# Mixed full and windowed attention on one core: transfer lists charged with measured issue times, lists of B's values queued only on a short SyncE backlog, and a new table of planner settings

## The chip, the cores and the metric

The kernel runs on one core of a Trainium2 chip. The metric is the device time of one execution in microseconds, lower is better. A core has a matrix engine (TensorE, PE in the profile), a vector engine (VectorE, DVE), an activation engine (ScalarE, ACT), GpSimd (POOL) and SyncE (SP), which here only issues DMA transfers. The engines run their own instruction lists and meet through semaphores.

## The reference

Two attentions over the same input x (2048 tokens, 640 features, bfloat16, 32 heads of 20 features) are mixed by a gate that is computed for each token. Attention A is full, without a mask; attention B lets every token see itself and seven earlier ones at distances 2, 4, ... 14.

```python
g = sigmoid((x * gate_w).sum(-1, keepdims=True))
# A: qkv = x @ A_wqkv;  p = softmax(q k^T * 20**-0.5);  a = (p v) @ A_wo
# B: qkv = x @ B_wqkv;  k, v gathered at pos - 2*w, w = 0..7 (masked below 0)
#    attn = softmax(q . k_w * 20**-0.5);  b = (sum_w attn_w v_w) @ B_wo
return g * a + (1 - g) * b
```

## The kernel before

**A planner writes the order.** The Python program that builds the kernel is a list scheduler. `_Sched.task` (called `T`) appends one instruction, or one list of DMA issues, to an engine's list and moves that engine's clock forward by a charged duration. For a DMA list it is given two charges: `dur`, after which the list's data are taken to be there, and `iss`, the time that SyncE is held by each of its `nd` issues (0.75 us where nothing is said). These charges never run on the chip. They only decide which instruction the planner puts next on which engine. On the chip each engine works through its list in that order and waits on semaphores where data are late.

**Attention A.** The work is 32 groups: 8 sets of four heads (q = 0 to 7) by 4 chunks of 512 queries. A group has 64 units, one for each of 16 blocks of 128 keys and each of the four heads. A unit is a score matmul (L1672), an exponential, and a matmul with V into `obank` (L1742). Units are put into tiles of two or three (`next_tile`, L1620), two tile buffers `score` taking turns. ScalarE computes the exponentials of a whole tile (`ebuf`, L1697). A tile of two can carry one more unit as a "ride": VectorE computes that exponential with integer arithmetic, first `uD` (L1687), and then, for four such units together, three shifted copies `eD` (L899). Both ways end in matmuls into `obank`. At the end of a group `gen_norm` transposes `obank` (L845), divides, and stores the result with a list of transfers `oTd<-oN` (L864).

**Side work.** Everything else is written as Python generators, which ask for a resource (`yield ("pe", ...)`, `("dve", ...)`, `("bank", ...)`) and are advanced by `step` (L1280) between two tiles, in `spend` (L1773), as far as the planner's clocks allow. `run_until` forces one of them forward where a tile needs its result. The generators that matter here:

- `gen_v` projects A's values, the first half of the heads in the order VORD, then the second half.
- `gen_q1` (L772) projects the queries of the first four heads for the query chunks 1 to 3. It writes |q| into `stg` (L783) as an input for a bound on the scores.
- `gen_kq` (L679) projects K and then Q for the other 28 heads in five shards f (six heads each, four in the last). For each shard: four K projections copied into `stg` (L698), a list of transfers into `kT` (L703), the largest |k| on VectorE (L707 to L718), four Q projections (L728), a list into `qT` (L733), and the bound from |q| and the largest |k| through `qbnd` into `qT` (L756). The weights of the next step are loaded into `WqP` by `w_load` (L674).
- `gen_bproj(u)` (L919) projects B's q, k and v for a unit u of 256 tokens (copies L945) and queues four lists of four transfers that spread v to the layout `vR` (L953).
- `gen_b(u)` (L958) multiplies q by k shifted (L971), sums, takes the softmax, sends the factors `rB` by transfers (L1054, L1056), multiplies the weights by `vR` (L1068), and sums into `oB`.
- `gen_wo` loads B's output weights (L604); `gen_fold` multiplies by the output weights and stores the result (L1259).

All these transfer lists go through SyncE's one queue, in the order in which the planner queued them. A list that waits for its data holds those behind it.

**The table.** `PLAN` holds a row of 18 settings for many tile numbers s (multiples of 5); from tile s on they hold until the next row. They are margins and priorities: how far a side matmul may run past a tile's limit (SLACK), when a third bank may be given to a tile (XTOL, XPRIO, XLATE), when VectorE may take a ride (DWAIT, DIDLE, DIDLE2, DTIME), the priorities of the shifted copies, how far VectorE may be booked ahead, when a filler matmul is put in (FILL), and how much earlier B's work is taken (BOFF). With other settings the order of the whole program is another.

Of the kernel before, what the change touches and what calls it, by code (L numbers as in the profile page):

```python
# [404 lines left out]
def _build(ctx, nc, A_x, A_wqkv, A_wo, B_wqkv, B_wo, gate_w, out):  # L405
# [266 lines left out]
    def w_load(part, f):  # L672
        d0, m = DH * heads[f][0], DH * len(heads[f])
        T("sp", 3.0, lambda e: e.dma_start(WqP[:, :, 0:m], wA_v[:, :, part * D + d0:part * D + d0 + m]), writes=WQ, dma=True)  # L674

    due = [99]
    kqn = [0]

    def gen_kq():  # L679
# [1255 lines left out]
```

## Time and profile before

| | before |
|---|---|
| median of 3 runs (lowest to highest) | 808.96 us (808.18 to 810.17) |
| profiled execution: time, span | 807.94 us, 806.1 us |
| granted TensorE clock, mean | 0.999 |
| TensorE busy | 746.2 us (93%) |
| VectorE busy | 741.8 us (92%) |
| ScalarE busy | 769.8 us (95%) |
| GpSimd busy | 92.5 us (11%) |
| exponentials on ScalarE, on VectorE | 1640 units in 725 tiles, 408 units |
| DMA | 32.6 MB, mean 40 GB/s |

The span runs from the first to the last instruction of the profiled execution; that execution's time is 1.84 us longer. An engine's idle time is the span less its busy time. Durations of instructions that follow one another on an engine overlap a little in the profile, so that the distance between starts can be shorter than the duration. A DMA list is seen on SP as so many issues; when it has landed is seen from the engine that waited for it.

### The profile page before, as it was taken

The numbers are of one execution on the slowest core, as the hardware profiler recorded it, in microseconds if no ns is written. First come the engines' busy times: TensorE is split into PE (matmuls) and PEld (weight loads), VectorE is DVE, ScalarE is ACT, GpSimd is POOL, SyncE is SP. The second block draws the span as 40 slices with busy tenths as digits, with TensorE's granted clock in tenths as the row PEclk, the third lists the DMA queues.
The fourth block names the chain that finished last, engine by engine and source line by source line (L and its number), as shares of the span: only waits on it lengthen the run. The fifth ranks groups of instructions, "written<-read, shape, count | busy, mean of one in ns | idle before, by whom it ended". The sixth has DMA issues, their size and how long they took to land.

```text
span 806.1 us, 27829 instructions
## 1 busy us (share of the span) xinstructions
PE 746.2 (93%) x11855; PEld 280.5 (35%) x11857; DVE 741.8 (92%) x1266; ACT 769.8 (95%) x757; POOL 92.5 (11%) x148
## 2 busy tenths in 40 slices
PE   8999998989999898989999998989899999999997
PEld 4323342334334233323343342333234333333322
DVE  7878998989999999999999999999999899999896
ACT  4999999989999999999999999999999999999996
POOL 3010001110020010101110100100021010111110
PEclk9999999999999999999999999999999999999999
DMA  8001110141030021101301320310212003000001
GB/s 261 26 24 31 26 33 6 38 85 29 6 76 11 5 44 38 22 22 40 76 13 38 78 54 22 74 27 6 64 28 65 5 17 81 22 23 23 23 21 35
DMA packets 47535, 32.61 MB, mean 40 GB/s; under 512 B 15029, under 2 KB 45653, under 8 KB 47413
## 3 DMA queue, kind: packets, MB, share of 16 engines
q1 hardware_dynamic: 47124, 30.51, 15.6%
q8 instruction: 94, 1.54, 0.8%
q10 hardware_dynamic: 288, 0.33, 0.1%
q14 instruction: 29, 0.23, 0.1%
HBM read 9.34 MB, written 2.62 MB: 15 GB/s over the span
## 4 chain that ended last, share of the span: by engine, by line
DVE 35%; PE 29%; ACT 15%; issue 10%; SPq 7%; DMA 3%; POOL 0%; POOLq 0%; DVEq 0%; ACTq 0%
ACT ebuf L1697 15%; DVE uD L1687 12%; PE score L1672 8%; PE obank L1742 8%; DVE eD L899 8%; PE side L651 7%; SPq L953 6%; DVE stage L971 3%; PE score L651 3%; DVE qkvB L945 2%; DVE stage L1068 2%; DMA stage<-qkvB 2%; DVE oTt L845 1%; DVE vA L814 1%; DMA qT<-stg 1%
## 5 line engine op out<-in xcount | busy, mean ns | idle before, releaser
L1697 ACT ACTIVATE ebuf<-score 128x1024 bf16<-128x1024 f32 (+1 forms) x725 | 758.1, 1184 | 19.6 <-PE score L1672 17.8
L1672 PE MATMUL score<-qT,kT 32*128 32x512 bf16 x2048 | 285.7, 384 | 31.5 <-ACT ebuf L1697 20.7
L1687 DVE TENSOR_SCALAR uD<-score 128x512 int16<-128x512 f32 x408 | 269.9, 682 | 17.1 <-PE score L1672 16.0
L899 DVE TENSOR_SCALAR eD<-uD 128x2048 int16<-128x2048 int16 x306 | 209.6, 706 | 3.8 <-PE obank L1742 3.0
L1742 PE MATMUL obank<-ebuf,vA 128*21 128x512 bf16 x1640 | 153.2, 385 | 9.5 <-DVE oTt L845 3.4
L1672 PEld LDWEIGHTS score<-qT,kT 32*128 32x128 bf16 x2048 | 70.7, 91 | 262.2 <-ACT ebuf L1697 172.0
L1742 PE MATMUL obank<-eD,vS 128*21 128x512 bf16 x1224 | 107.7, 380 | 1.2 <-DVE eD L899 1.2
L651 PE MATMUL side<-xT,wBs 128*32 128x256 bf16 x2400 | 96.2, 281 | 1.7 <-DVE qkvB L945 1.2
L851 POOL TENSOR_TENSOR rcp<-rcp,gA 128x16 f32<-128x16 f32 x31 | 7.5, 243 | 659.6 <-DVE rcp L849 659.6
L651 PEld LDWEIGHTS side<-xT,wBs 128*32 128x32 bf16 x2400 | 68.4, 142 | 29.7 <-issue 14.5
L1742 PEld LDWEIGHTS obank<-ebuf,vA 128*21 128x21 bf16 x1640 | 36.7, 89 | 92.6 <-issue 57.5
L1068 DVE TENSOR_TENSOR stage<-stage,eB 128x2048 bf16<-128x2048 bf16 x40 | 48.0, 1224 | 6.2 <-DMA stage<-qkvB 6.2
L651 PE MATMUL side<-xT,WqP 128*32 128x512 bf16 (+2 forms) x605 | 48.5, 382 | 2.0 <-DVE qkvB L945 0.9
L971 DVE TENSOR_TENSOR stage<-qkvB 128x2048 bf16<-128x2048 bf16 x40 | 47.8, 1230 | 0.1
L945 DVE CAST qkvB<-side 128x512 bf16<-128x512 f32 (+1 forms) x72 | 42.1, 594 | 3.0 <-PE side L651 2.8
L1742 PE MATMUL obank<-uD,vA 128*21 128x512 bf16 x408 | 39.6, 379 | 0.0
L890 POOL TENSOR_TENSOR vS<-vA,vw 128x252 bf16<-128x252 bf16 x55 | 37.0, 693 | 19.1 <-DVE maskB L594 13.2
L1742 PEld LDWEIGHTS obank<-eD,vS 128*21 128x21 bf16 x1224 | 29.9, 91 | 21.2 <-DVE eD L899 4.0
L858 POOL TENSOR_TENSOR oN<-oTt,rcp 128x512 bf16<-128x512 f32 x31 | 32.7, 1054 | 2.4
L845 DVE STREAM_TRANSPOSE oTt<-obank 128x512 f32<-128x512 f32 x32 | 22.8, 712 | 4.8 <-PE obank L1742 4.6
L651 PE MATMUL side<-xT,oTd 128*32 128x512 bf16 (+1 forms) x500 | 26.1, 304 | 0.0
L651 PEld LDWEIGHTS side<-xT,WqP 128*32 128x32 bf16 (+2 forms) x605 | 13.1, 94 | 19.8 <-issue 7.9
(200 smaller groups left out, 477.0 us busy)
## 6 DMA issues: line engine op xcount, KB each, us to landing
stage<-qkvB SPq DMA_DIRECT2D x128, 80.6 KB, 2.1
wBs<-in_B_wqkv_dram SPq DMA_DIRECT2D x1, 2400.0 KB
kT<-stg SPq DMA_DIRECT2D x28, 80.0 KB
qT<-stg SPq DMA_DIRECT2D x28, 80.0 KB
oTd<-oN SPq DMA_DIRECT2D x108, 20.0 KB
out_dram<-outsb SPq DMA_DIRECT2D x12, 160.0 KB
oTd<-in_A_x_dram SPq DMA_DIRECT2D x2, 640.0 KB
WqP<-in_A_wqkv_dram SPq DMA_DIRECT2D x8, 150.0 KB, 2.5
```

Source lines behind the costliest of these rows:

```text
L651: ins = e.matmul(o[j:k, :], l(j) if callable(l) else l[:, j:k], r, start=(first and i == 0), stop=(last and i == n - 1), skip_group_check= ...
L858: T(en, c2, lambda e: e.tensor_tensor(oo, ii, ib, ALU.mult), reads=["rcp", "oTt"], writes=["oN0"])
L890: T("pool", 0.607, lambda e: e.tensor_tensor(vS[:, i, :, :], _ap(vA[q // 4], (kb * 4 + q % 4) * 4 * DV, [[0, K - 1], [1, 4 * DV]]), _ap(vw ...
L899: T("dve", 0.065 + 0.1334 * n, lambda e, k=k, sl=sl: e.tensor_scalar(eD[:, sl % NS, 0:512 * n].bitcast(I16), uD[d % NU][:, 0:512 * n].bitc ...
L945: t = TB(dvc(n * TOK), lambda e, o=o, i=i: e.tensor_copy(o, i), reads=[("side", b)], writes=[key])
L953: T("sp", 2.0 + 0.65 * 4, lambda e, w4=w4, lo=lo: [e.dma_start(vR[32 * w4:32 * w4 + 32, a * CN:(a + 1) * CN, :], vB[32 * a:32 * a + 32, :, ...
L971: TB(dvc(CH, 2), lambda e: e.tensor_tensor(o, i0, i1, ALU.mult), reads=["qB", "kB"], writes=[("prod", i)] + ([("WkP", 0)] if u == 0 else [ ...
L1068: TB(dvc(CH, 2), lambda e: e.tensor_tensor(o, i0, i1, ALU.mult), reads=["eB"] + [("vR", w4) for w4 in range(4)], writes=[("prod", i)], por ...
L1672: ins = e.matmul(o, kT[32 * j:32 * j + 32, q % NQS, kb * P:(kb + 1) * P], qT[32 * j:32 * j + 32, q % NQS, GROUPS[g][0] * 512:(GROUPS[g][0] ...
L1687: t = T("dve", 0.598, lambda e: e.tensor_scalar(uD[d % NU][:, 512 * i:512 * (i + 1)].bitcast(I16), side[x], UOFF, 0.0, op0=ALU.add, op1=AL ...
L1697: exps[s] = T("act", actc(512 * n), lambda e: e.activation(ebuf[s % NE][:, 0:512 * n], score[s % 2][:, 0:512 * n], ACTF.Exp, scale=LN2 / S ...
L1742: ins = e.matmul(obank[32 * j:32 * j + DV, :], v, src, start=(kb == 0), stop=(last and k >= len(lst) - 4), skip_group_check=True)
```

## The change

It has five parts.

1. **Charges.** `dur` and `iss` of the transfer lists of `gen_kq`, of `vR`, of `rB` and of B's output weights get other numbers.
2. **WkQ.** K's weights of shard 0 are loaded at the start into a free part of `stage`. `gen_kq` begins when the first half of V and the query chunk 1 are projected (before: when all query chunks of `gen_q1` are). After the K half of shard 0 it waits for `gen_q1` to end, and goes on with Q, whose weights `gen_q1` loads last in place of K's. `gen_q1` uses `qbnd` for |q|, as `stg` is in use by then. `gen_b` waits for shard 0's K half, since its first product overwrites `WkQ`.
3. **The gate on vR lists.** Before each of the four lists `gen_bproj` asks for SyncE: the list is queued only when SyncE's planned backlog is at most 0.4 us.
4. **Order of B's projections.** The projection of v for unit u waits until the vR lists of unit u - 1 are queued.
5. **The table.** All rows of `PLAN` are replaced (its last row is at tile 725; before, at 720).

```diff
 PLAN = {
-    0: ((0.31, 0.76), 0.01, 1.0, 5.5, 0.94, -1.37, -0.5, 9.99, 7.0, 5.87, 0.67, 0.62, 5.69, 4.3, 0.0, 0.63, 2, -3),
...
-    720: ((0.34, 0.86), 0.16, 1.0, 5.5, 0.94, -1.14, -0.97, 9.86, 7.0, 8.62, 0.59, 0.62, 5.69, 5.04, 0.0, 0.54, 2, -3),
+    0: ((0.32, 0.64), 0.16, 2.5, 2.5, 0.94, -1.41, -0.97, 11.8, 7.0, 8.62, 0.67, 0.96, 4.4, 4.3, 0.0, 0.75, 2, -3),
...
+    725: ((0.48, 0.45), 0.25, 2.5, 5.5, 0.83, -2.18, -0.5, 5.48, 2.0, 6.06, 0.52, 0.47, 4.61, 3.44, 0.2, 0.52, 2, 0),
 }
...
# gen_wo
-              writes=[("woBp", f)] + (...), dma=True, iss=3.7)
+              writes=[("woBp", f)] + (...), dma=True)
...
+    WkQ = _ap(stage, 1024, [[DH * len(heads[0]), CN], [1, DH * len(heads[0])]])
+    T("sp", 3.0, lambda e: e.dma_start(WkQ, wA_v[:, :, D + DH * heads[0][0]:D + DH * heads[0][0] + DH * len(heads[0])]),
+      writes=["WkQ"], dma=True)
...
# gen_kq
-        while not done.get(("q", POS[QCN - 1, 0])):
+        while not (done.get(("v", VORD[-1], 0)) and done.get(("q", POS[1, 0]))):
             yield ("cond",)
         for f in range(CN):
+            Wk, wk = (WkQ, ["WkQ"]) if f == 0 else (WqP, WQ)
...
-                mms = [(side[b][0:m, :], WqP[:, c, 0:m], xT[:, c, cols]) for c in range(CN)]
-                yield from mm_group(b, mms, WQ + XT(tcc), mmc(512))
-                if tcc == 3:
+                mms = [(side[b][0:m, :], Wk[:, c, 0:m], xT[:, c, cols]) for c in range(CN)]
+                yield from mm_group(b, mms, wk + XT(tcc), mmc(512))
+                if tcc == 3 and f:
                     w_load(0, f)
...
# lists kT<-stg and qT<-stg
-            T("sp", 2.2 + 0.65 * len(hs), ... iss=0.65)
+            T("sp", 2.7 + 0.765 * len(hs), ... iss=0.765)
...
# after the K half of a shard
+            done[("k", f)] = True
+            while not done.get(("q", POS[QCN - 1, 0])):
+                yield ("cond",)
...
# list qT<-qbnd
-            T("sp", 2.2 + 0.65 * 4 * len(runs), ... iss=0.65)
+            T("sp", 2.4 + 0.55 * 4 * len(runs), ... iss=0.55)
...
# gen_q1
-                w_load(1, 0)
+                w_load(0, 0)
...
-                stg[:, cols].bitcast(U16), side[b][:, :].bitcast(U16)[:, 1:1024:2], 0x7FFF, None, op0=ALU.bitwise_and),
-              reads=[("side", b)], writes=[("stg", qc)])
-            yield from mm_group(b, [(side[b][:, :], KM[0], stg[:, cols])], [("KM", 0), ("stg", qc)], mmc(512), first=False)
+                qbnd[:, :].bitcast(U16), side[b][:, :].bitcast(U16)[:, 1:1024:2], 0x7FFF, None, op0=ALU.bitwise_and),
+              reads=[("side", b)], writes=["qbnd"])
+            yield from mm_group(b, [(side[b][:, :], KM[0], qbnd[:, :])], [("KM", 0), "qbnd"], mmc(512), first=False)
...
# gen_bproj
+            while u and m == 2 and f0 == 0 and not done.get(("bproj", u - 1)):
+                yield ("cond",)
...
         for w4 in range(4):
+            yield ("sp", 0.4)
             lo = PADB - DIL - 2 * DIL * w4
-            T("sp", 2.0 + 0.65 * 4, lambda e, w4=w4, lo=lo: [e.dma_start(
+            T("sp", 3.2 + 0.65 * 4, lambda e, w4=w4, lo=lo: [e.dma_start(
...
# gen_b
-        while not (done.get(("bqk", u)) and (u == 0 or done.get(("bs", u - 1)))):
+        while not (done.get(("k", 0)) and done.get(("bqk", u)) and (u == 0 or done.get(("bs", u - 1)))):
             yield ("cond",)
...
# lists of rB
-        T("sp", 2.0 + 0.5 * 4, ...
+        T("sp", 2.4 + 0.65 * 4, ...
-        spread = lambda: T("sp", 2.0 + 0.5 * 3, ...
+        spread = lambda: T("sp", 2.4 + 0.65 * 3, ...
...
# step
+        elif req[0] == "sp":
+            if not force and sch.avail["sp"] > now + req[1]:
+                return False
```

More of the change, by code (lines that the diff above doesn't have):

```diff
@@ L604, in gen_wo @@
             T("sp", 6.0, lambda e, f=f, src=src: e.dma_start(woBp[f], src) if f < CN - 1 else e.dma_start(woBp[f][:, :], src),
-              writes=[("woBp", f)] + ([("vA", kb, 0) for kb in range(KBN)] + [("vAones", 0)] if f == 0 else []), dma=True, iss=3.7)
+              writes=[("woBp", f)] + ([("vA", kb, 0) for kb in range(KBN)] + [("vAones", 0)] if f == 0 else []), dma=True)
             n = nchunk[0]
@@ L702, in gen_kq @@
             old = [k_ for q in qs if q >= NQS for tcc in range(4) for k_ in kT_keys(q - NQS, tcc)]
-            T("sp", 2.2 + 0.65 * len(hs), lambda e, hs=hs: [e.dma_start(
+            T("sp", 2.7 + 0.765 * len(hs), lambda e, hs=hs: [e.dma_start(
                 kT[32 * (h % 4) + 1:32 * (h % 4) + 1 + DH, h // 4 % NQS, :], stg[DH * i:DH * i + DH, :]) for i, h in enumerate(hs)],
-              reads=SG + [("kTz", q) for q in qs if q < NQS], writes=[("kTd", q, f) for q in qs] + old, dma=True, nd=len(hs), iss=0.65)
+              reads=SG + [("kTz", q) for q in qs if q < NQS], writes=[("kTd", q, f) for q in qs] + old, dma=True, nd=len(hs), iss=0.765)
             yield ("dve", DVE_AHEAD, sch.free(*SG))
@@ L732, in gen_kq @@
             old = [k_ for q in qs if q >= NQS for qc in range(QCN) for k_ in qkeys[POS[qc, q - NQS]]]
-            T("sp", 2.2 + 0.65 * len(hs), lambda e, hs=hs: [e.dma_start(
+            T("sp", 2.7 + 0.765 * len(hs), lambda e, hs=hs: [e.dma_start(
                 qT[32 * (h % 4) + 1:32 * (h % 4) + 1 + DH, h // 4 % NQS, :], stg[DH * i:DH * i + DH, :]) for i, h in enumerate(hs)],
-              reads=SG + [("qTz", q) for q in qs if q < NQS], writes=[("qTd", q, f) for q in qs] + old, dma=True, nd=len(hs), iss=0.65)
+              reads=SG + [("qTz", q) for q in qs if q < NQS], writes=[("qTd", q, f) for q in qs] + old, dma=True, nd=len(hs), iss=0.765)
             yield ("dve", DVE_AHEAD, sch.free(*SG))
@@ L755, in gen_kq @@
             runs = [(q, [i for i, h in enumerate(hs) if h // 4 == q]) for q in qs]
-            T("sp", 2.2 + 0.65 * 4 * len(runs), lambda e, runs=runs, hs=hs: [e.dma_start(
+            T("sp", 2.4 + 0.55 * 4 * len(runs), lambda e, runs=runs, hs=hs: [e.dma_start(
                 qT[32 * (hs[il[0]] % 4):32 * (hs[il[-1]] % 4) + 1:32, q % NQS, qc * 512:(qc + 1) * 512],
@@ L759, in gen_kq @@
               reads=["qbnd"] + [("qTz", q) for q in qs if q < NQS], writes=[("qTb", q, f) for q in qs] + old, dma=True,
-              nd=4 * len(runs), iss=0.65)
+              nd=4 * len(runs), iss=0.55)
             for q in qs:
@@ L951, in gen_bproj @@
         for w4 in range(4):
+            yield ("sp", 0.4)
             lo = PADB - DIL - 2 * DIL * w4
-            T("sp", 2.0 + 0.65 * 4, lambda e, w4=w4, lo=lo: [e.dma_start(
+            T("sp", 3.2 + 0.65 * 4, lambda e, w4=w4, lo=lo: [e.dma_start(
                 vR[32 * w4:32 * w4 + 32, a * CN:(a + 1) * CN, :], vB[32 * a:32 * a + 32, :, lo:lo + VW]) for a in range(4)],
-              reads=["vB"], writes=[("vR", w4)] + ([("WkP", 0)] if u == 0 and w4 == 0 else []), dma=True, nd=4, iss=0.65)
+              reads=["vB"], writes=[("vR", w4)], dma=True, nd=4, iss=0.65)
         done[("bproj", u)] = True
@@ L971, in q_chunk @@
             TB(dvc(CH, 2), lambda e: e.tensor_tensor(o, i0, i1, ALU.mult),
-               reads=["qB", "kB"], writes=[("prod", i)] + ([("WkP", 0)] if u == 0 else []), port=True)
+               reads=["qB", "kB"], writes=[("prod", i)] + ([("WkP", 0), "WkQ"] if u == 0 else []), port=True)
         def q_sum(f, b):
@@ L1052, in gen_b @@
            reads=["rQ", "tB"], writes=["rQ"])
-        T("sp", 2.0 + 0.5 * 4, lambda e: [e.dma_start(rB[0:32, j * TQ:(j + 1) * TQ], rQ[32 * j:32 * j + 32, :]) for j in range(4)],
+        T("sp", 2.4 + 0.65 * 4, lambda e: [e.dma_start(rB[0:32, j * TQ:(j + 1) * TQ], rQ[32 * j:32 * j + 32, :]) for j in range(4)],
           reads=["rQ"], writes=["rB"], dma=True, nd=4)
-        spread = lambda: T("sp", 2.0 + 0.5 * 3, lambda e: [e.dma_start(rB[32 * i:32 * i + 32, :], rB[0:32, :]) for i in range(1, 4)],
+        spread = lambda: T("sp", 2.4 + 0.65 * 3, lambda e: [e.dma_start(rB[32 * i:32 * i + 32, :], rB[0:32, :]) for i in range(1, 4)],
                            reads=["rB"], writes=["rB"], dma=True, nd=3)
```

262 rows, old and new, of the table PLAN are left out of this document.

## The prediction

> **What bounds the kernel now.** I read part 1 of the page first, then the groups of instructions by shape, then busy time in stretches of 50 us, then the waits of ScalarE and VectorE, and last the timeline around the longest wait.
>
> ```profile
> PE 746.2 (93%) x11855; PEld 280.5 (35%) x11857; DVE 741.8 (92%) x1266; ACT 769.8 (95%) x757; POOL 92.5 (11%) x148
> ```
>
> Three engines are over 90% busy; ScalarE is the fullest, and the span is its 769.8 us of work plus 36.3 us of idle time. Its work is nearly all exponentials:
>
> ```profile
> L1697 ACT ACTIVATE ebuf<-score 128x1024 bf16<-128x1024 f32 x533 | 512.6, 1072 | 13.1 <-PE score L1672 11.6
> L1697 ACT ACTIVATE ebuf<-score 128x1536 bf16<-128x1536 f32 x191 | 271.5, 1500 | 6.6 <-PE score L1672 6.2
> ```
>
> 533 tiles of two units, 191 of three and a single unit make 1640 of the 2048 units; the other 408 go to VectorE (uD, L1687). A unit taken from a tile of three is worth 1500 - 1072 = 428 ns to ScalarE. So time can come only from idle time, or from units that VectorE takes over. Where is the idle time?
>
> ```profile
> core 0: us, PE busy (x) PEld busy (x) DVE busy (x) ACT busy (x) POOL busy (x), PEclk, DMA share, GB/s
> ...
> 50.00:100.00 50.00, 49.85 (x700) 15.44 (x692) 44.79 (x80) 49.87 (x52) 3.69 (x6) 1.00 0.11 24
> 100.00:150.00 50.00, 46.46 (x727) 17.27 (x728) 44.79 (x78) 47.14 (x49) 3.68 (x6) 1.00 0.11 23
> 150.00:200.00 50.00, 45.08 (x759) 18.26 (x747) 45.73 (x78) 47.27 (x47) 4.54 (x8) 1.00 0.26 57
> 200.00:250.00 50.00, 46.72 (x784) 19.22 (x784) 48.43 (x80) 49.55 (x52) 6.14 (x10) 1.00 0.16 34
> ```
>
> Of the 36.3 us, 14.6 lie before 50 us (start-up) and 8.4 after 750 (the drain). The fourteen stretches between leave 13.3 us: in order 0.13, 2.86, 2.73, 0.45, 0, 0.41, 0.10, 0.40, 0.49, 1.65, 0, 0.94, 1.27, 1.85. Two of them, 100 to 200 us, hold 5.6. Their largest single piece has a transfer behind it (timeline):
>
> ```profile
> 169.81 2.55 SPq L953 DMA_DIRECT2D stage<-qkvB  x4
> ...
> 175.56 1.23 DVE L1068 TENSOR_TENSOR stage<-stage,eB 128x2048 bf16<-128x2048 bf16 x1 [2.69 <-DMA stage<-qkvB]
> 176.71 0.71 DVE L845 STREAM_TRANSPOSE oTt<-obank 128x512 f32<-128x512 f32 x1
> ...
> 177.56 0.61 PE L1742 MATMUL obank<-ebuf,vA 128*21 128x512 bf16 x8 [1.96 <-DVE oTt L845]
> ...
> 178.76 1.45 ACT L1697 ACTIVATE ebuf<-score 128x1536 bf16<-128x1536 f32 x1 [2.26 <-PE score L1672]
> ```
>
> The reader sees one late list stop three engines in turn: VectorE waits 2.69 us for the last vR list, the transpose of obank behind it is late, TensorE waits for that, and ScalarE idles 2.26 us. The planner had put the multiplication there because it took the list for done. VectorE's waits say how much there is of this kind:
>
> ```profile
> DVE stage L1068 <- DMA stage<-qkvB: 6.2, 6, 2.7
> DVE stg L737 <- DMA qT<-stg: 1.0, 2, 0.7
> ```
>
> (The columns: us in all, times, longest.) 7.2 us of VectorE in the whole run, of which only the piece above is longer than 1.1 us.
>
> **Part by part.** The sum is made against the profiled execution: span 806.1, time 807.94, so 1.84 lies around the span. The median of the three runs, 808.96, is 1.02 above that execution.
>
> *The charges.* A vR list of four issued from 169.81 released VectorE at 175.54, after 5.73 us; before charges 2.0 + 4 x 0.65 = 4.6, after 5.8. The qT list issued from 99.47 was done at 103.26 + 3.52 = 106.78, after 7.31; before charges 2.2 + 6 x 0.65 = 6.1, after 2.7 + 6 x 0.765 = 7.29. The bound rows issued eight in 4.71 and 4.36 us, 0.54 to 0.59 each; charged 0.65 before, 0.55 after. A load of B_wo is issued in 0.6 us; before holds SP for 3.7, after for 0.75. The new charges thus meet the rows within 0.1 us or so a piece, and an engine is no longer placed 1.2 us ahead of its data. What that is worth to ScalarE: the 2.26 us at 178.76, since the other waits lie beside idle times of 0.8 us at most. Behind it TensorE's side work is late next: ScalarE's other gaps in these 100 us, 0.20 to 0.91 us each, all wait for scores behind projections. All of it is counted in the stretches below.
>
> [...]
>
> *WkQ, the early load.* One more issue before wBs: 0.38 us (L674's median). SP ends gwT's issue at 8.37 and sits until 13.39 for x's last transpose, so it is covered; uncovered it would make wBs 0.38 late, which is first read at 105 us. Its 150 KB take 0.6 us at the 261 GB/s of the first slice, behind the x loads: 0 to 0.6, taken 0, as it is queued last. One load fewer comes later (shard 0's K weights), so ten stay ten.
>
> *Shard 0's K half moves up.* Four projections at 1.19 us of TensorE (20 matmuls, the chain's row) are 4.8 us; on VectorE four copies of 0.69, the absolute value 0.73, folds 0.82 + 0.48 + 0.36, maximum 0.42, KMd 0.23: 5.8 us; on SP six issues, 4.5 us. They start when V's first half ends (47.5 us) in place of q1's end (60.7), some 13 us earlier. Nothing of it is added. The Q weights' load, issued at 76.3 after the K projections, can now go at 60.7, so Q's list (99.5) and the bound's list (110.1 to 114.8) can come up to 15 us earlier, ahead of B's first projections (105 to 121), which now crowd TensorE exactly where ScalarE loses 2.86 us. Worth 0 to 2.9; which part goes is in the stretches below.
>
> *q1's |q| through qbnd* keeps its instruction (0.69 us); the two uses at 51.3 and 58.95 lie 7.6 us apart, so the single buffer costs nothing.
>
> *The gate on vR lists.* Sixteen issues took 11.0 to 11.6 us in one go. With a backlog limit of 0.4 the next list is asked for when the charged 2.6 us of the last have run down to 0.4; alone on the queue, they stay about as dense. If another list slips between, vR is later by 2.5 (rB), 3.6 (oTd) or 4.5 us (kT, qT), and what waits on SP behind is the rest of vR, then rB's spread; L1068 waits for both. Eight units at 4.5 would be 36 us at most, spread over a B chain that runs from 115 to 697 us with 105 us to spare before the drain. Cost 0 (one list of 4.5 us standing between VectorE and its data if that slack were gone); the V projections' new condition on the lists of the unit before falls away with it, as those are queued a unit earlier.
>
> *The new table.* Every wait above disappears only if the new order puts other work there, and the trace of before cannot show that order. I bound it by stretches. Floor: all fourteen at their median, 0.47: 13.3 - 6.6 = 6.7 us saved. Other side: as uneven as now but drawn afresh; the fourteen have a standard deviation of 0.98, and the sum of fourteen draws one of 0.98 x 3.74 = 3.7 us, so up to +3.7. I take the two stretches whose cause is named down to the median: 5.59 - 0.94 = 4.7 saved, nearest to the floor because the five stretches right after them average 0.27.
>
> *VectorE's freed time.* A unit costs VectorE 0.60 (the pitch of uD in runs) and three shifted copies of 0.60 per four units, 1.05 us in all. The 2.69 us stall holds two, worth 0.86 to ScalarE; all 7.2 us would hold six or seven, 2.9. I take 0.9, since pieces under 1.1 us hold no whole unit.
>
> Sum: 4.7 + 0.9 = 5.6. Span 806.1 - 5.6 = 800.5, execution 802.3, median 803.4. The forecast's own range: best 6.7 + 2.9 = 9.6 saved, 799.4; least, the 2.26 alone, 806.7.
>
> **Rivals.**
> *1. The waits move.* ScalarE and TensorE wait on each other through two score buffers (TensorE's weight loads waited 172 us for ebuf), and VectorE already has 64 us idle; removing 7.2 of it may only lengthen other gaps. For: the trace shows five of six transfer waits with little ScalarE idle beside them. Against: the 2.26 us. Gain 0 to 2: 807 to 809.
> *2. Slower: the K half in a full stretch.* From 47.5 to 80 us TensorE is busy 31.8 of 32.5 us, with no filler matmul in it (L1763 shows none before 80). If the 4.8 us of projections are taken there between V and the remaining q1 and are then not deferred, ScalarE loses up to 4.8 at 47 to 75 us, and what falls free at 100 us comes back only as the 2.9 it idles there. It decides if the K work is placed while scores are due, that is if ScalarE's idle between 50 and 100 us passes 3 us (0.13 now). With nothing else gained: 808.96 + 4.8 - 2.3 = 811.5; without the 2.3, 813.8. Against: side work is normally let in only where it ends before the next tile's limit.
> *3. Slower: the draw.* The new table is merely another draw of the same quality on the unlucky side, +3.7: 812.7. Against: its charges fit the rows better than the old.
> *4. The charges were right as they stood*, the lists being done 2.1 us after their last issue, as the column of landings says: then the recharging only holds work back, and the early K half is left, 0 to 2.9: 806 to 809. [...]
>
> **How the numbers follow.** About 0.3%, 2.4 us, is what a measurement of this kernel tells from no change. Forecast 0.58; rival 1 0.14, rival 4 0.04, rival 2 0.14, rival 3 0.10. Faster: 0.58 plus 0.03 of rivals 1 and 4 at their low ends, 0.61. Same: the remaining 0.15. Slower: 0.24. Range: downward the best case and half a draw (1.8), 797.5; upward through rival 3's 812.7, leaving out the worst of rival 2. The likeliest case alone: 799 to 807.
>
> **What would show it.** Right: VectorE's wait at L1068 for stage<-qkvB under 2 us in all; the kT list starting before 65 us and the bound's list before 105; ScalarE's idle 100 to 200 us near 1 us; some 410 to 415 uD units. The gate shows as vR issues in groups of four with other lists between. Wrong: ScalarE's idle between 50 and 750 us at 13 us or more, wherever it moved; or over 3 us between 50 and 100 us (rival 2); or fewer than 408 units on VectorE, which would add 0.43 us of ScalarE work each.

## The result, and the profile after

| | before | after |
|---|---|---|
| median (lowest to highest) | 809.57 us (808.18 to 811.38, 4 runs) | 802.05 us (800.37 to 803.12, 4 runs) |
| ratio | | 0.9901, interval 0.9877 to 0.9925 |
| profiled execution: time, span | 807.94, 806.1 us | 802.65, 800.8 us |
| its granted clock | 0.999 | 0.995 |

The kernel is 7.5 us faster in the medians and 5.3 us in the two profiled executions; 803.4 and a span of 800.5 were forecast. A later set of four runs of the changed kernel on another chip gave 801.10 us against 808.41 (0.9913, 0.9897 to 0.9928); its profiled execution took 800.99 us, with a span of 799.2.

Part 1 of the page of the changed kernel, and its exponentials among the groups by shape (count, then busy us and mean ns, then idle time before them):

```profile
PE 753.1 (94%) x11881; PEld 281.0 (35%) x11881; DVE 738.2 (92%) x1259; ACT 770.7 (96%) x761; POOL 91.9 (11%) x147
```
```profile
L1712 ACT ACTIVATE ebuf<-score 128x1024 bf16<-128x1024 f32 x543 | 520.6, 1065 | 9.2 <-PE score L1687 8.3
L1712 ACT ACTIVATE ebuf<-score 128x1536 bf16<-128x1536 f32 x186 | 264.4, 1496 | 4.4 <-PE score L1687 4.1
L1702 DVE TENSOR_SCALAR uD<-score 128x512 int16<-128x512 f32 x404 | 266.8, 680 | 19.9 <-PE score L1687 19.6
```

ScalarE did not get less to do: 404 units ride on VectorE where 408 did, and ScalarE's busy time rose from 769.8 to 770.7 us. The gain is idle time: the span less the busy time fell from 36.3 to 30.1 us. Busy time in stretches of 50 us tells where (the ACT column). First the start of the kernel before, then the changed kernel:

```profile
0.00:50.00 50.00, 44.13 (x600) 20.27 (x606) 37.13 (x93) 35.44 (x36) 9.22 (x17) 1.00 0.39 122
```
```profile
core 0: us, PE busy (x) PEld busy (x) DVE busy (x) ACT busy (x) POOL busy (x), PEclk, DMA share, GB/s
0.00:50.00 50.00, 47.09 (x649) 20.96 (x649) 37.52 (x93) 37.75 (x40) 9.22 (x17) 1.00 0.42 127
50.00:100.00 50.00, 48.93 (x640) 14.76 (x642) 41.10 (x74) 49.45 (x54) 3.30 (x5) 1.00 0.14 31
100.00:150.00 50.00, 46.76 (x687) 16.25 (x685) 48.42 (x85) 49.62 (x51) 4.69 (x7) 1.00 0.08 19
150.00:200.00 50.00, 48.54 (x799) 19.21 (x796) 47.60 (x81) 49.74 (x51) 6.82 (x11) 1.00 0.23 49
...
700.00:750.00 50.00, 47.25 (x751) 15.18 (x751) 43.14 (x73) 47.14 (x47) 7.40 (x11) 0.97 0.06 19
```

| stretch (us) | ScalarE idle before | after | change | forecast |
|---|---|---|---|---|
| 0 to 50 | 14.56 | 12.25 | -2.3 | 0 |
| 50 to 100 | 0.13 | 0.55 | +0.4 | 0 |
| 100 to 200 | 5.59 | 0.64 | -5.0 | -4.7 |
| 200 to 750 | 7.56 | 8.77 | +1.2 | 0 |
| after 750 | 8.4 | 7.9 | -0.4 | 0 |
| ScalarE's busy time | 769.8 | 770.7 | +0.8 | -0.9 |

The sum is -5.3, the difference of the spans. This is one execution of each kernel. In the profiled execution of the later set the changes are -1.8, +0.4, -5.0, -0.8, -0.4 and +0.5 in the same order, -6.9 in all: the stretch of 100 to 200 us and the direction at the start come again, the loss between 200 and 750 us does not.

VectorE's wait for vR, 6.2 us in 6 before, is all but gone (waits: us in all, times, longest), and SyncE's timeline shows the early K half (the kT list at 64.51, the bound's at 100.72) and the gate, which lets another list in between vR lists in two of the eight units:

```profile
DVE stage L1080 <- DMA stage<-qkvB: 0.3, 1, 0.3
```
```profile
64.51 4.53 SPq L709 DMA_DIRECT2D kT<-stg  x6
...
100.72 4.33 SPq L765 DMA_DIRECT2D qT<-qbnd  x8
...
653.83 9.41 SPq L965 DMA_DIRECT2D stage<-qkvB  x12
663.27 3.58 SPq L873 DMA_DIRECT2D oTd<-oN  x4
666.96 0.90 SPq L1271 DMA_DIRECT2D out_dram<-outsb  x2
667.95 2.66 SPq L965 DMA_DIRECT2D stage<-qkvB  x4
```

In the chain of work that ended last, the queue and the transfers, 10% before (SPq 7%, DMA 3%), have left:

```profile
PE 44%; DVE 27%; ACT 18%; issue 10%; SPq 0%; DMA 0%; DVEq 0%; ACTq 0%
```

### The profile page after: what moved, and what is told of

Its sections match the earlier page's. It is cut to its first block, busy times and chain, and to the rows that moved or that the text cites. A ratio compares the mean times of both kernels' runs of the same rounds, so it can differ in the third digit from the quotient of the medians.

```text
span 800.8 us, 27867 instructions
## 1 busy us (share of the span) xinstructions
PE 753.1 (94%) x11881; PEld 281.0 (35%) x11881; DVE 738.2 (92%) x1259; ACT 770.7 (96%) x761; POOL 91.9 (11%) x147
## 4 chain that ended last, share of the span: by engine, by line
PE 44%; DVE 27%; ACT 18%; issue 10%; SPq 0%; DMA 0%; DVEq 0%; ACTq 0%
ACT ebuf L1712 18%; PE score L1687 13%; PE obank L1757 12%; PE side L653 11%; DVE uD L1702 8%; DVE eD L908 6%; PE score L653 3%; DVE stage L983 3%; DVE qkvB L956 2%; DVE stage L1080 1%; DVE oTt L854 1%; PE side L1090 1%; PE score L1395 1%; DVE oN L870 1%; DVE stg L704 0%
## 5 line engine op out<-in xcount | busy, mean ns | idle before, releaser
L1687 PE MATMUL score<-qT,kT 32*128 32x512 bf16 x2048 | 288.6, 386 | 27.5 <-ACT ebuf L1712 18.8
L1702 DVE TENSOR_SCALAR uD<-score 128x512 int16<-128x512 f32 x404 | 266.8, 680 | 19.9 <-PE score L1687 19.6
L908 DVE TENSOR_SCALAR eD<-uD 128x2048 int16<-128x2048 int16 x303 | 206.1, 705 | 3.5 <-PE obank L1757 2.8
L1757 PE MATMUL obank<-ebuf,vA 128*21 128x512 bf16 x1644 | 156.4, 387 | 2.3 <-DVE oTt L854 0.8
L1757 PE MATMUL obank<-eD,vS 128*21 128x512 bf16 x1212 | 105.7, 380 | 0.7 <-DVE eD L908 0.7
L653 PE MATMUL side<-xT,WqP 128*32 128x512 bf16 (+2 forms) x550 | 44.5, 383 | 1.7 <-DVE stg L704 1.0
L653 PE MATMUL score<-WvH,xT 128*32 128x320 bf16 x400 | 21.0, 301 | 0.0
```

Source lines behind the costliest of these rows:

```text
L653: ins = e.matmul(o[j:k, :], l(j) if callable(l) else l[:, j:k], r, start=(first and i == 0), stop=(last and i == n - 1), skip_group_check= ...
L908: T("dve", 0.065 + 0.1334 * n, lambda e, k=k, sl=sl: e.tensor_scalar(eD[:, sl % NS, 0:512 * n].bitcast(I16), uD[d % NU][:, 0:512 * n].bitc ...
L1687: ins = e.matmul(o, kT[32 * j:32 * j + 32, q % NQS, kb * P:(kb + 1) * P], qT[32 * j:32 * j + 32, q % NQS, GROUPS[g][0] * 512:(GROUPS[g][0] ...
L1702: t = T("dve", 0.598, lambda e: e.tensor_scalar(uD[d % NU][:, 512 * i:512 * (i + 1)].bitcast(I16), side[x], UOFF, 0.0, op0=ALU.add, op1=AL ...
L1757: ins = e.matmul(obank[32 * j:32 * j + DV, :], v, src, start=(kb == 0), stop=(last and k >= len(lst) - 4), skip_group_check=True)
```

## The experiments

Each ratio is to the kernel before on the same chip. Its medians: 808.67 us beside A to D, 808.75 beside K1, G2 and D2, 807.20 beside E2 and F, 808.41 beside the last three (H and the two repeats).

### The code and the table, each alone

`a_newcode_oldtable` is the changed kernel with the old rows of `PLAN`; `b_oldcode_newtable` is the kernel before with the new rows. The theory was that a table is tied to the code and the charges that it was searched for; the rivals were that one of the two halves is better by itself.

> The code of after (charges, early K half, gate) with before's table of settings. My theory: a table was searched for one code and one set of charges, so the order made with the other is a fresh draw; it lands at 806 to 822 us, without the 7.5 us of the change, and ScalarE's idle time between 50 and 750 us is 13 us or more. Rival 'the code itself is better': the early K half and the right charges remove the transfer waits and the idle time of 100 to 200 us under any table, 802 to 806 us. Either way VectorE's wait for vR at L1080 should stay under 2 us, since that hangs on the charges.

> Before's code and charges with the new table. My theory: again a draw, 806 to 822 us, with VectorE's wait for vR back at 4 us or more, as the old charges come 1.2 us early. Rival 'the table itself is better': 800 to 805 us whatever the charges.

Measured: A 848.44 us, ratio 1.0489 (1.0460 to 1.0518); B 865.49 us, 1.0694 (1.0666 to 1.0723). Both are far slower than either whole kernel: the theory had the direction, but both sizes are missed by tens of us. In A VectorE does not wait for vR at all, yet ScalarE's wait for scores is 43.3 us. In B, where the old charges should have brought 4 us or more of waits for vR, there are 1.1 us in 2: how much of this wait there is hangs on the order as a whole, not on the charges alone. The first long stall of A, on its timeline (idle time and releaser in brackets):

```profile
133.06 0.61 PE L1685 MATMUL score<-qT,kT 32*128 32x512 bf16 x3 [6.15 <-DMA qT<-qbnd]
...
133.71 2.37 ACT L1710 ACTIVATE ebuf<-score 128x1536 bf16<-128x1536 f32 x2 [8.73 <-PE score L1685]
```

The old rows, with the new code, put the bound's list so late (127.68 us; 110.09 in the kernel before, 100.72 in the changed one) that the next group's scores stand for it. So these rows are worth something only with the code that they were searched for, and the change is not a sum of "code" and "table". Charges, early K half and gate were not taken apart here.

One part does carry over. In B, with the old code, ScalarE is busy 37.47 us in the first 50 us; in A, with the new code, 35.09 (before: 35.44, after: 37.75):

```profile
0.00:50.00 50.00, 46.99 (x642) 21.07 (x644) 37.71 (x94) 37.47 (x40) 9.20 (x17) 1.00 0.39 124
```
```profile
0.00:50.00 50.00, 44.14 (x595) 20.54 (x601) 37.02 (x92) 35.09 (x36) 9.20 (x17) 1.00 0.40 124
```

(First B, then A.) The gain of the start-up thus belongs to the table's first rows, with either code. Its size differs between executions: over the kept profiles ScalarE is busy 34.9 to 35.7 us with the old rows and 36.9 to 37.8 with the new ones.

### The late list taken away by hand

`c_before_vr0_first` is the kernel before, where on SyncE alone one list changes place: unit 0's four vR lists go ahead of the oTd list that had stood before the first of them. Nothing else moves.

```diff
+    l_ = sch.lists["sp"]
+    i_ = l_.index(vrt[0])            # vrt: the vR lists, in order
+    l_.insert(i_ + 3, l_.pop(i_ - 1))
```

> Before, every engine's order kept but SyncE's: the four vR lists of unit 0 go ahead of the one list oTd<-oN that they stood behind, so they start when v is copied (157.4 us) and not at 161.0, 3.6 us earlier. My theory: the 2.69 us wait of VectorE at 175.56 goes, with it ScalarE's 2.26 us at 178.76, and the span falls by 2.3 us (2 to 2.5). Rival 'waits move': ScalarE's idle appears elsewhere and the span changes by less than 0.5 us.

Measured: 806.04 us, 0.9964 (0.9946 to 0.9981), 2.6 us faster; 2.3 were forecast. The multiplication that waited 2.69 us no longer does, the ScalarE tile behind it starts with a gap of 0.15 us where 2.26 were, and the stretch of 150 to 200 us loses 2.2 of its 2.7 idle us; the one before it (2.4 idle) hardly changes. C's waits by VectorE, a line of its timeline, and the two stretches:

```profile
DVE stage L1071 <- DMA stage<-qkvB: 2.2, 3, 1.2
```
```profile
173.21 2.37 ACT L1700 ACTIVATE ebuf<-score 128x1536 bf16<-128x1536 f32 x2 [0.15 <-PE score L1675]
```
```profile
100.00:150.00 50.00, 47.00 (x753) 17.80 (x751) 45.49 (x78) 47.60 (x50) 3.68 (x6) 1.00 0.11 24
150.00:200.00 50.00, 46.69 (x766) 18.59 (x763) 48.38 (x83) 49.50 (x50) 4.74 (x9) 1.00 0.25 55
```

So the stall at 175 us was worth about its whole length, and the first 2.3 us of the prediction's sum are shown with it, as far as the interval goes (1.5 to 4.4 us). The two profiled executions alone would have said 5.0 us (802.91 for 807.94); the rest of that lies in other stretches.

### Lists late on purpose

Is a late vR list always that dear? The theory put the price of D at 1 to 5 us; the rival had it hidden. In the changed kernel, `d_after_late_vr` issues the last vR list of each unit as six transfers in place of four (1.3 us more on SyncE), and `d2_after_vr8` all four lists as eight each (the last then some 11 us late). The planner's charges are unchanged.

```diff
# d_after_late_vr (in d2: "for f0, f1 in ((0, 2), (2, CN))" in every list)
-    vR[..., a * CN:(a + 1) * CN, :], vB[..., :, lo:lo + VW]) for a in range(4)]
+    vR[..., a * CN + f0:a * CN + f1, :], vB[..., f0:f1, lo:lo + VW])
+    for a in range(4) for f0, f1 in (((0, 2), (2, CN)) if w4 == 3 and a > 1 else ((0, CN),))]
```

> After, every engine's order kept, but the last vR list of each of the eight units is issued as six transfers (two of the four split in half, same bytes), so that it is done about 1.3 us later than planned: the size of the old charge's error. My theory: VectorE's waits for vR come back, 3 to 8 us in all from 0.3, and the time rises by 1 to 5 us. Rival 'such waits are hidden': VectorE's waits may rise, but the time stays within 1 us.

> After, every engine's order kept, every vR list issued as eight transfers (each of the four split in two, same bytes): the last list of a unit ends about 11 us later than planned. The large dose beside the run with 1.3 us. My theory: with the slack of 1 to 3 us used up, VectorE waits 6 to 10 us in most of the eight units, 40 to 70 us in all, ScalarE gets three quarters of it as idle time, and the time is 30 to 55 us longer. Rival 'B has slack': VectorE's waits stay under 15 us in all and the time under 6 us longer.

Measured: D 802.19 us, 0.9914 (0.9888 to 0.9940): within what can be told as fast as the changed kernel, against my theory; its waits of 2.5 us are also fewer than the 3 to 8 expected. D2 878.88 us, 1.0863 (1.0810 to 1.0915). VectorE's waits in D and then in D2, and ScalarE's in D2:

```profile
DVE stage L1081 <- DMA stage<-qkvB: 2.5, 3, 1.0
```
```profile
DVE stage L1081 <- DMA stage<-qkvB: 57.0, 8, 10.1
```
```profile
ACT ebuf L1713 <- PE score L1688: 84.2, 47, 9.9
```

In D three waits, 0.59, 1.00 and 0.96 us, cost too little for the times to show it (the interval is 2 us to either side). The trace shows something: ScalarE's gaps some 4 and 7 us behind the two longer ones (397.65 and 599.83 us) are 0.73 and 1.27 us, where the changed kernel has none and 0.87, so 1.1 us more. In D2 eight waits of up to 10.1 us, 57.0 together as forecast (40 to 70), cost 77 us of time where I had put three quarters of them or less: ScalarE's waits for scores grew by 72 us, more than VectorE's by 57. The granted clock, 0.953 on the mean against 0.995, may hold a part of the surplus; its share was not separated. So the price of a wait was not in proportion to its length here: up to 1 us at most half of it was found in the trace, at 2.7 us about all of it in C, and with eight waits of up to 10 us more than all of it.

### The other gaps between 100 and 150 us

The prediction blamed B's first projections for 2.86 us of gaps there. `k1_before_thin_b0` is the kernel before with unit 0's projections on 64 of their 256 columns, and `e2_before_late_bound` is the kernel before with shard 0's bound list issued as 16 transfers in place of 8, which takes away the slack that the early K half is to add.

```diff
# k1
+    TK = TOK if u else 64
-    mms = [(side[b][:, k * TOK:(k + 1) * TOK], ..., xT[:, c, t0:t0 + TOK]) ...
+    mms = [(side[b][:, k * TOK:k * TOK + TK], ..., xT[:, c, t0:t0 + TK]) ...
# e2
+    for c0, c1 in (((0, 256), (256, 512)) if hs[0] == 4 else ((0, 512),))
```

> Before, every engine's order kept, but B's projections of unit 0 (TensorE, L651, 105 to 121 us and again near 155) compute 64 of their 256 columns, so about three quarters of their matmul time is left out. My theory of the idle time of ScalarE at 100 to 130 us: TensorE is crowded there by these projections. Then ScalarE's 2.86 us between 100 and 150 us fall below 1.2 and the time falls by 1.5 to 3 us. Rival 'group 4 waits for its queries and bounds, or for VectorE': the 2.86 stays within 0.5 us and so does the time.

> Before, every engine's order kept, but the list that carries shard 0's bound into qT (L756, from 110 us) is issued as sixteen transfers instead of eight (each split in half, same bytes), so it ends some 4.4 us later, at about 121 in place of 117. Group 4, the first to read it, starts near 123. My theory after the last runs: the early K half brought slack that nothing had waited for, so the time stays within 1 us of before. Rival 'the first shard's lists were at the edge, and their earlier start is what freed 100 to 150 us': ScalarE waits 2 us or more at 120 to 127 us and the time rises by 2 us or more.

Measured: K1 809.05 us, 0.9993 (0.9972 to 1.0014), with 2.45 us idle there in place of 2.86: TensorE is busy 1.6 us less from 100 to 150 us (44.87 for 46.46), and one gap, at 124 us, shrinks from 0.57 to 0.25 us, but the others stay, and my cause fell. E2 807.87 us, 1.0009 (0.9995 to 1.0023), the same gaps: the bound's list 4.0 us longer on SyncE (8.71 for 4.71) costs nothing that the run could tell, so an earlier bound was not being waited for in the old order. What two of the gaps do wait for is on the timeline of the kernel before:

```profile
124.16 1.94 ACT L1697 ACTIVATE ebuf<-score 128x1024 bf16<-128x1024 f32 x2 [0.57 <-PE score L1672]
...
125.26 0.72 DVE L845 STREAM_TRANSPOSE oTt<-obank 128x512 f32<-128x512 f32 x1
...
126.03 0.61 PE L1742 MATMUL obank<-ebuf,vA 128*21 128x512 bf16 x8 [0.61 <-DVE oTt L845]
...
127.01 1.94 ACT L1697 ACTIVATE ebuf<-score 128x1024 bf16<-128x1024 f32 x2 [0.91 <-PE score L1672]
```

This is the end of a group: the matmuls into obank wait until VectorE has transposed it, the scores queued behind them on TensorE are late, and ScalarE idles 0.91 us. The other gap of 0.91 us, at 102.43, lies behind the group end before (transpose at 99.35); there TensorE does not wait, but has two microseconds of other matmuls, projections for the gate and the first ones into obank, ahead of the scores. The gap of 0.57 stands behind matmuls that waited for VectorE's shifted copies (0.28 us at 122.75). In the changed kernel the transposes are at 99.15 and 121.87 us, and ScalarE runs through both, without a gap from 94.50 to 127.99 us; the second part of this run:

```profile
110.24 17.75 ACT L1712 ACTIVATE ebuf<-score 128x1024 bf16<-128x1024 f32 x15
```

So 1.8 of the 2.5 us gained in this stretch are gaps at or behind group ends that the new order does not have; that this is the cause is read from the two timelines and was not tested by a run. Which part of the change let the order be found, the early K half among them, stays open: an order searched anew for each part alone was not run.

### The gate alone

`g2_after_vr_dense` is the changed kernel with the four vR lists of a unit next to each other on SyncE again. Only the two units differ in which another list had come between.

```diff
+    for u in range(2 * QCN):
+        four = vrt[4 * u:4 * u + 4]
+        for t_ in four[1:]: l_.remove(t_)
+        i_ = l_.index(four[0]); l_[i_ + 1:i_ + 1] = four[1:]
```

> After, every engine's order kept but SyncE's: the four vR lists of a unit stand together again where another list had slipped in (two of the eight units). My theory: no difference, within 1 us of after, as VectorE reads vR later anyway. Rival 'the gate pays because it lets other lists through': 2 us or more slower, with a new wait of VectorE or of SP's readers behind those lists.

Measured: 805.18 us, 0.9952 (0.9932 to 0.9971), 3 to 4 us slower than the changed kernel (802.05 and 801.10): the rival held. I had costed the gate at nothing; it earns its place in one unit. G2's SyncE and what follows:

```profile
655.73 12.07 SPq L966 DMA_DIRECT2D stage<-qkvB  x16
...
671.10 0.90 SPq L1273 DMA_DIRECT2D out_dram<-outsb  x2
...
673.08 0.69 DVE L1258 CAST outsb<-side 128x512 bf16<-128x512 f32 x1 [2.82 <-DMA out_dram<-outsb]
...
673.83 0.61 PE L653 MATMUL side<-vA,oB 128*32 128x512 bf16 x8 [1.79 <-DVE outsb L1258]
...
674.95 1.02 ACT L1714 ACTIVATE ebuf<-score 128x1024 bf16<-128x1024 f32 x1 [1.68 <-PE score L1689]
```

The stores of the result come 15.4 us after the start of the vR lists, where it was 13.1 in the changed kernel (671.10 after 655.73, and 666.96 after 653.83), so sixteen issues in one go put them 2.2 us later. The next copy into `outsb` needs that buffer: VectorE waits 2.82 us at it (0.65 in the changed kernel), TensorE waits for VectorE, and ScalarE idles 1.68 us. Before this place G2's execution runs 2.0 us behind the other, after it 4.1 (ScalarE's tiles at 651.34 for 649.37 and at 692.20 for 688.08): the stall is worth 2.1 us. The 2.0 us before it are not the gate's: 1.8 of them arose from 200 to 250 us, ahead of the first list that was moved, at a clock of 0.93. Why the medians differ by 1 to 2 us more than the stall was not settled; G2's clock (0.9955 in the middle of twelve executions) is also lower than the changed kernel's (0.9975 in the middle of eight). In the other unit (265 to 279 us) the two are equal (ScalarE busy 49.45 and 49.47 us from 250 to 300). It is the stall of 175 us over again, with another list as the one held up.

### Filling TensorE's gaps

The executions of one kernel differ, among other things, in their mean granted clock (0.990 to 1.000 in the 17 executions of the kernel before beside H), which drops in places (last section). `f_after_fed` adds 54 groups of four matmuls of zeros into the open obank of the changed kernel where the planner leaves TensorE over 0.45 us unused; `h_before_vr0_fed` adds 78 such groups to C. `after_again` and `f_again` are the changed kernel and F together on one chip.

```diff
+    if open_ and gap > 0.45:     # in TensorE's finished list
+        for _ in range(int((gap - 0.2) / 0.22)):
+            out_.append(_Task(-1, "pe", "cmp", pad, []))   # pad: 4 matmuls, zero x ident into obank
```

> After, every engine's order kept, but 54 extra matmuls of zeros into the open obank (0.22 us each, 12 us of TensorE in all) in the places where the planner itself leaves TensorE idle for more than 0.45 us. In the traces the granted clock falls to 0.5 for one stretch of about 3.4 us where TensorE had been busy 2.2 to 2.7 us of the 3.4 us before, and the executions of one kernel differ by such drops. My theory: the drops are a part of what idle time costs; with TensorE fed the granted clock stays at 0.998 or more in the median run (after: 0.9965) and the median time is 1 to 2.5 us below after's. Rival 'the fillers stand in the way of scores': the clock rises, but ScalarE waits more for scores, and the time is the same or up to 3 us more.

> Before with the two repairs that keep its order: unit 0's vR lists ahead of the oTd list (worth 2.6 us in c_before_vr0_first) and 78 extra matmuls of zeros where the planner leaves TensorE idle for more than 0.45 us. What is left between this and f_after_fed is the order itself: 2.3 us at the start (new rows up to tile 45), 2.5 us between 100 and 150 us, less what after gives back after 700 us. My theory: 803 to 805 us, median clock 0.998 or more. Rival 'the gain of after is the clock and the one stall': 800 to 801.5, level with f_after_fed.

> After, unchanged, on the same chip as the two below, so that the run with the extra matmuls can be set against it and not only against before. Both theories expect 802 us and a median granted clock of 0.996 to 0.997.

> The kernel of f_after_fed once more, beside after on one chip. My theory (drops of the clock cost after 1 to 2.5 us): 1 to 2.5 us below after. Rival 'the difference of 1.8 us was one of chips': within 0.5 us of after.

Measured: F 800.25 us, 0.9913 (0.9891 to 0.9935), and again 800.09, 0.9902 (0.9884 to 0.9921); the changed kernel beside the second 801.10, 0.9913 (0.9897 to 0.9928). F is the fastest version run, 1.0 us under the changed kernel on one chip, but the intervals overlap: suggestive, not settled. H 806.02, 0.9971 (0.9949 to 0.9993), outside of both theories (803 to 805, 800 to 801.5) and the same as C without the fill (806.04), although its median clock is 0.998 as expected. With C's stall repaired and the gaps filled, the old order still stands 4.9 us behind the changed kernel and 5.9 behind F.

## Why the prediction was right, point by point

**The named stall: right.** The 2.26 us at 178.76 went: in the new order unit 0's vR lists are issued later, from 181.59 to 193.70 us, but the first multiplication stands only at 197.25, and 0.3 us of waits are left in the whole run. C shows the stall alone, at 2.6 us. That the new charges did this is what the planner was meant to do and was not shown by itself: with the old charges and the new rows (B) the waits are 1.1 us.

**The stretch of 100 to 200 us: right in size, half right in cause.** 4.7 forecast, 5.0 measured. The half from 150 to 200 us has the predicted cause. The half from 100 to 150 us has not: K1 made unit 0's projections a quarter as wide and all but 0.4 of the 2.86 us stayed. The step "B's first projections (105 to 121), which now crowd TensorE exactly where ScalarE loses 2.86 us" is wrong, and so is the reading that all gaps of these 100 us stand "behind projections": the one at 127 us stands behind the transpose of obank. Of the early K half's "0 to 2.9" E2 shows that the bound's list gave nothing in the old order. By the timelines the gain came at the group ends, where the new order has no gap.

**The new table: a term missing and a term too wide.** I let the table act only where a wait was named, and took the start-up's idle time as fixed. It fell by 2.3 us (1.8 in the later execution), and A and B show that it is the table's. From 200 to 750 us 1.2 us went the other way, which I had bounded by a draw of 3.7 but not priced. That was this execution: two drops of the clock lie in it, one with a gap of 1.15 us (438 us, below) and one near 735 us, and in the later execution ScalarE idles 6.8 us there, 0.8 less than before. The draw's own estimate, the spread of stretches of a tuned order, says nothing of an order that was not searched: A and B lie 40 and 57 us off.

**VectorE's freed time: wrong sign.** 0.9 us was to come from two more units on VectorE. There are four fewer, and ScalarE has 0.8 us more work; "fewer than 408 units on VectorE" stood among the prediction's signs of being wrong. Freed time became less VectorE work (738.2 for 741.8 us busy), not more rides.

**The gate: mis-sized.** Costed at 0, with the risk put at VectorE's wait for vR. G2 measures 3 to 4 us in its favour, of which 2.1 are traced to a list that I had not followed: the output's stores, behind which the copy into `outsb` stands. What I had called the cover ("105 us to spare") was the slack of vR, not that of the lists behind it.

The misses in the gain (+2.3 us at the start, -0.4 from 50 to 100 us, +0.3 in the next two stretches, -1.2 later, +0.4 at the end, -1.7 of busy time) nearly cancel, so 5.6 us came out as 5.3. That the sum is so near is luck: one term was rightly sized with half its cause, and the others made up for each other. The two profiled executions of the changed kernel stand 5.3 and 6.9 us under the one of before, the medians 7.5 and 7.3. Part of the difference goes with the clock. Straight lines through the recorded times (74 executions of the kernel before, 8 of the changed one) rise by some 0.7 and 0.3 us for each 0.001 of mean clock lost, with much scatter, and are 5.0 us apart at a clock of 1.000 (805.6 and 800.6). The kernel before also had the lower clock on the average (0.9957 for 0.9973), which by the same lines is the other 2 us between the averages. Such lines show that a low clock and a long time go together, not which brings the other.

**The rivals.** *The waits move*: fell, ScalarE's idle from 50 to 750 us is 10.0 us (13.3 before). *The K half in a full stretch*: fell, its mark was 3 us of idle from 50 to 100 us and 0.55 are there. *The draw*: fell for this order. *The charges were right as they stood*: fell, its time was 806 to 809 and 802.05 was measured; and its premise, a landing 2.1 us after the issue (the median on the page of before), fails in the trace of before, where these lists released their readers 3.78, 3.90, 3.17 and 3.16 us after the last issue in four cases of the chain and 2.13 us in one. What the new charges alone are worth was not measured.

## What to carry to other kernels

Charge a transfer list by its issues and by the measured time from its last issue to the release of its reader (here 3.16 to 3.90 us in four cases of five), and mend first the one wait behind which several engines stand: here 2.69 us of waiting were worth about 2.6 us of time, while three waits of up to 1 us were too small for the times to show. When a long run of issues is queued on a shared queue, follow every list behind it to the engine that waits for its buffer; the list that pays may be the output's store. Settings that were searched for one version of the code have to be searched again for the next, and a part of such a change can't be priced by leaving the others out: the two halves here cost 40 and 57 us alone. Profile a kernel more than once before explaining a difference of a microsecond: G2's and the changed kernel's profiles both held gaps that were not there in another execution.

## What the runs showed of the hardware that was not expected

In the changed kernel's profile the granted clock dropped to 0.50 for some 3.4 us (435.2 to 438.6 us) after TensorE had been only partly idle. Three stretches of 3.4 us around it (the column after POOL's is the clock), then the timeline:

```profile
431.40:434.80 3.40, 2.53 (x31) 0.65 (x28) 3.37 (x7) 3.40 (x4) 0.00 (x0) 1.00 0.09 22
434.80:438.20 3.40, 3.15 (x25) 0.62 (x25) 2.77 (x6) 2.25 (x4) 0.00 (x0) 0.56 0.22 55
438.20:441.60 3.40, 2.92 (x35) 0.74 (x33) 3.27 (x8) 3.40 (x4) 0.22 (x1) 0.94 0.01 3
```
```profile
435.05 0.51 PE L1687 MATMUL score<-qT,kT 32*128 32x512 bf16 x3 [0.95 <-ACT ebuf L1712]
...
437.98 2.37 ACT L1712 ACTIVATE ebuf<-score 128x1024 bf16<-128x1024 f32 x2 [1.15 <-PE score L1687]
```

TensorE was busy 2.53 of 3.40 us (74%), its longest idle piece, at the end of this stretch, was 0.95 us, and the stretch behind ran at 0.56; ScalarE idled 1.15 us at its end. In K1 a stretch of 65% (273 to 277 us) was followed by 0.51. In the kernel before two of 65% and 61%, around the stall at 175 us, were not followed by any drop; in K1 the same stall, in a stretch of 56%, was, by stretches at 0.66, 0.50 and 0.83, which add up to some 6.9 us at half the clock. From 220 to 225 us TensorE was busy 4.17 of 5 us in the changed kernel and 4.18 in G2 and in F, and the clock was 1.00, 0.74 and 0.80. So the same place is hit in one execution and not in another, and the busy share of such a stretch alone does not tell: one of 74% was followed by a drop and one of 61% was not. What sets off a drop was not found. With a drop behind it the same stall went with more idle time: from 150 to 200 us ScalarE idled 4.49 us in K1 and 2.73 in the kernel before. D2 (57 us of waits, 77 us of time, clock 0.953) is consistent with it, but the clock's share was not measured by itself there.
